# Other starting places in on-chip memory for two groups of operands of a packed attention and feed-forward kernel

## The chip, the core and the metric

The kernel runs on one core of a Trainium2 chip. Its time is the device time of one execution in microseconds (us). Three executions took 693.35, 694.07 and 694.8 us, so the median is 694.07 us. The core has a matrix engine (TensorE, PE in the profile; its weight loads have a row of their own, PEld), a vector engine (DVE), a scalar engine (ACT), a general engine (POOL) and a queue engine (SP), which here only starts transfers.

## What is computed

The inputs are q, k and v of 8 batches, 8 heads, 576 tokens and 64 values a head, 32 "pack" vectors p a head, and the matrices W_in (512 x 2048) and W_out (2048 x 512), all in 32 bits.

```
p_packed = softmax(scale * p @ k.T) @ v              # 32 rows a head
attn     = softmax(scale * q @ p_packed.T) @ p_packed
x        = attn with the heads side by side          # 4608 x 512
h        = x @ w_in
g        = h * (1 / (1 + exp(-h)))                   # SiLU
out      = g @ w_out                                 # 4608 x 512
```

The softmax adds 1e-9 to its sum. Nothing in the change touches the arithmetic.

## The kernel before

The second attention and W_in are merged. For each batch the pack vectors are first multiplied with W_in (the "packs times W_in", tiles `pw_hi` and `pw_lo`), and the hidden values h then come from the softmax shares `a2` times those. Every 32-bit operand of a large product is split into an upper part that TensorE's float32r type holds exactly and the lower remainder, and a product takes three matmuls: upper by upper, upper by lower, lower by upper.

Three kinds of matmul carry nearly all the work. Each is preceded by its own load of 128 columns of a stationary operand (128 x 128 values, 512 bytes in each partition), while the moving operand is streamed past it:

- **h, line 590.** 12 matmuls for a unit of two column blocks. The stationary operand is a slice of `pw_hi` or `pw_lo`, the moving one 288 columns of `a2_hi` or `a2_lo`. A tile of the packs has two halves, one for the even heads and one for the odd (`par` 0 and 1 in the code), each of 512 values. In a group of six matmuls the first three use half 0 and the last three half 1.
- **out, pairs, line 648 with 128 x 256.** For batches 2 to 7 the product with W_out is done by a scheme with seven products instead of eight for a pair of column blocks (`pair_products`). The stationary operands are seven parts of g (`g_hi` and `g_lo`, 7 x 128 values), the moving ones 256 columns of W_out or of sums of its blocks. A unit has 7 x 3 = 21 matmuls, and there are 96 units.
- **out, plain, line 648 with 128 x 512.** The first two batches use g without pairs, and the last 32 tokens of every half (the "rests") do so in all batches.

For a pair ACT writes g from PSUM (line 612), POOL makes the sums and differences (lines 622 to 624), ACT writes the upper parts (`all_upper`, line 638), DVE the lower parts (`all_lower`, line 642), and then TensorE may go on. A string, ORDER, sets the order of these steps on PE, DVE, ACT and SP by hand. A step named `Z0.` closes the pools of the early part and opens `pw_b` and `gp_main`, in which all g of the pairs lies.

Where a tile lies is set by the order in which pools are opened and by their sizes. I call the distance of an operand's first byte from the multiple of 256 bytes below it its *place*. All pools up to `gp_main` have sizes that are multiples of 256 bytes, at least between the big tiles, and so the tiles of W_out, of its sums, of the packs and of g itself begin at place 0. The slices that are used as operands are 512, 1024 or 2048 bytes apart and have the place of their tile. There are two exceptions: the second half of an `a2` tile begins 1152 bytes into it, at place 128; and `all_upper` puts the upper and lower parts of the pairs 56 values into their tile, at place 224 (for the rests it puts them at 0):

```
at = AT_G if g.shape[1] > FJ * P else 0          # line 634, AT_G = 56
both = [gp_main.tile([P, 7 * P + 64], F32R, name=name) for name in ("g_hi", "g_lo")]
```

Of the kernel before, what the change touches and what calls it, by code (L numbers as in the profile page):

```python
# [9 lines left out]
F32 = mybir.dt.float32  # L10
F32R = mybir.dt.float32r
# [8 lines left out]
P = 128  # L20
# [11 lines left out]
JW = DFF // NJ  # L32
FJ = JW // P
# [88 lines left out]

TP_BUFS = 4
EDGE = 504
AT_G = 56
ON_TOKENS = (0,)
SCALE = 1.0 / math.sqrt(D)
EPS = 1e-9
# [5 lines left out]
def packed_attention_ffn(ctx: ExitStack, tc: tile.TileContext, pkT, qT, v, w_in, w_out, out):  # L134
# [14 lines left out]
    ent = ctx.enter_context  # L149
    const = ent(tc.tile_pool(name="const", bufs=1))  # L150
    kvq = ent(tc.tile_pool(name="kvq", bufs=2))
    pw = ent(tc.tile_pool(name="pw", bufs=2))
# [29 lines left out]
    made = {}  # L182
# [39 lines left out]
    class Weights:  # L222
# [51 lines left out]
        def upper(self, n):  # L274
            hi, _ = self.both(n)
            nc.scalar.copy(hi, self.raw[n][1].bitcast(F32))
# [250 lines left out]
    class Packs:  # L527
# [18 lines left out]
        def upper(self):  # L546
            b, j = self.b, self.f // FJ
            if self.f % FJ == 0:
                pool = pw_b if b >= EARLY and j >= 2 else pw
                made["pw", b, j] = [pool.tile([P, 2, JW], F32R, name=name) for name in ("pw_hi", "pw_lo")]  # L550
            c = slice(self.f % FJ * P, (self.f % FJ + self.nf) * P)
            self.hi, self.lo = (t[:, :, c] for t in made["pw", b, j])
            nc.scalar.copy(self.hi, self.ps[:, :, : self.nf * P])
# [72 lines left out]
    def all_of(u):  # L626
        b, f, *more = units[u]
        if more:
            return rest[:, f : f + FJ].rearrange("p f e h s -> p (f e h s)")
        return hidden[u][:, P:]  # L630

    def all_upper(u):
        g = all_of(u)
        at = AT_G if g.shape[1] > FJ * P else 0
        both = [gp_main.tile([P, 7 * P + 64], F32R, name=name) for name in ("g_hi", "g_lo")]
        both = [t[:, at : at + g.shape[1]] for t in both]
        hidden[u] = g, *both
        nc.scalar.copy(both[0], g)  # L638
# [160 lines left out]
    def load_parts(b):  # L799
# [38 lines left out]
        "N": rest_values,  # L838
        "I": pair_sums,
        "F": all_upper,  # L840
        "L": all_lower,
        "O": lambda u: (rest_products if len(units[u]) > 2 else pair_products)(u),
# [13 lines left out]
    def early_done():  # L856
        nonlocal pw_b, gp_main
        scope.close()
        at_right[1].close()
        pw_b = ent(tc.tile_pool(name="pw_b", bufs=2, reuse_waits="tile"))  # L860
        gp_main = ent(tc.tile_pool(name="gp_main", bufs=2, reuse_waits="tile"))

    def weights_done():
# [7 lines left out]

    pw_b = gp_main = ring = tp = None
    steps |= {"Z0.": early_done, "Z1.": weights_done}
    for step in ORDER.split():
        which = step.rstrip("0123456789.") if step[0] != "Z" else step
# [44 lines left out]
```

## Time and profile before

| | |
|---|---|
| median of three executions | 694.07 us (693.35 to 694.8) |
| the profiled execution | 693.81 us, of which 692.0 us are the profile's span |
| TensorE busy | 672.5 us, 97% |
| DVE busy | 425.8 us, 62% |
| ACT busy | 387.0 us, 56% |
| POOL busy | 233.6 us, 34% |
| the chain that ended last | PE 76%, DVE 10%, ACT 5%, DMA 3% |

Durations of matmuls in the profile overlap: a matmul's row runs on while the next one has begun. How fast a stream of them goes is therefore read from starts in the timeline, or from the pieces of the chain of waits, which are merged by line and have a length and a count. A mean duration is of use only for comparing like with like.

### The profile page before, as it was taken

How to read it: one execution, taken by the hardware profiler on the slowest of the kernel's cores; microseconds unless marked ns; L12 is line 12 of the kernel's file. 1: busy time of each engine (PE TensorE's matmuls, PEld its weight loads, DVE VectorE, ACT ScalarE, POOL GpSimd, SP SyncE). 2: the span in 40 equal slices, each digit the busy share in tenths (PEclk: the TensorE clock that was granted, in tenths of full speed). 3: DMA queues.
4: the chain of work that ended last, by engine and by line, in shares of the span. 5: the costliest groups of instructions: out<-in, count | busy, mean ns of one | idle time of the engine just before them, and what ended most of it. 6: DMA issues, size and time to landing. Idle time of an engine off the chain costs nothing.

```text
span 692.0 us, 14725 instructions
## 1 busy us (share of the span) xinstructions
PE 672.5 (97%) x5958; PEld 591.5 (85%) x5958; DVE 425.8 (62%) x588; ACT 387.0 (56%) x641; POOL 233.6 (34%) x336
## 2 busy tenths in 40 slices
PE   7799999999999999999999999999999999999997
PEld 5477776788878998999888998899888898899995
DVE  5989989896774536753666425853665535663333
ACT  5787887463645535663556634755554754664431
POOL 1102054343203432544423343353251353435520
PEclk9899999999999999999999999999999999999999
DMA  9848864685967678967797578874994848685531
GB/s 362 328 136 307 282 222 173 235 267 184 386 242 283 247 245 329 363 251 262 283 342 282 184 284 308 348 279 131 353 353 168 303 132 307 265 313 190 212 139 45
DMA packets 55107, 178.62 MB, mean 258 GB/s; under 512 B 21760, under 2 KB 25856, under 8 KB 47360
## 3 DMA queue, kind: packets, MB, share of 16 engines
q1 hardware_dynamic: 54944, 177.56, 69.1%
q8 instruction: 47, 0.77, 0.4%
q10 hardware_dynamic: 96, 0.13, 0.1%
q14 instruction: 20, 0.16, 0.1%
HBM read 149.42 MB, written 24.12 MB: 251 GB/s over the span
## 4 chain that ended last, share of the span: by engine, by line
PE 76%; DVE 10%; ACT 5%; DMA 3%; issue 2%; POOL 2%; SPq 1%; ACTq 0%; DVEq 0%
PE ps_acc L648 45%; PE ps_two L590 23%; PE ps_two L287 5%; DMA win<-in_w_out 2%; PE ps_two L387 2%; DVE tm L423 1%; DVE g_lo L642 1%; DMA sums_of_w<-sums_of_w 1%; DVE g_lo L608 1%; DVE w_raw L252 1%; ACT g_hi L638 1%; DVE w_raw L256 1%; ACT g L612 1%; DVE wo_lo L280 1%; POOL g L623 1%
## 5 line engine op out<-in xcount | busy, mean ns | idle before, releaser
L642 DVE TENSOR_TENSOR g_lo<-g,g_hi 128x896 fp32r<-128x896 f32 x96 | 105.9, 1110 | 131.6 <-ACT g_hi L638 131.2
L648 PE MATMUL ps_acc<-wo_hi,g_hi 128*128 128x256 f32 (+1 forms) x576 | 184.7, 321 | 0.7 <-DVE o L790 0.7
L648 PE MATMUL ps_acc<-wo_hi,g_lo 128*128 128x256 f32 (+1 forms) x576 | 183.0, 318 | 2.2 <-DVE g_lo L608 2.2
L648 PE MATMUL ps_acc<-wo_lo,g_hi 128*128 128x256 f32 (+1 forms) x576 | 182.7, 317 | 0.0
L590 PE MATMUL ps_two<-a_hi,pw_hi 128*128 128x288 f32 x512 | 153.0, 299 | 1.5 <-DVE tm L423 1.5
L622 POOL TENSOR_TENSOR g<-g 128x128 f32<-128x128 f32 x96 | 56.2, 586 | 288.0 <-ACT g L612 287.9
L590 PE MATMUL ps_two<-a_lo,pw_hi 128*128 128x288 f32 x512 | 151.3, 295 | 0.0
L590 PE MATMUL ps_two<-a_hi,pw_lo 128*128 128x288 f32 x512 | 151.1, 295 | 0.0
L638 ACT CAST g_hi<-g 128x896 fp32r<-128x896 f32 x96 | 89.9, 942 | 77.6 <-POOL g L624 47.5
L648 PEld LDWEIGHTS ps_acc<-wo_hi,g_hi 128*128 128x128 f32 x576 | 108.1, 188 | 16.1 <-issue 5.6
L648 PEld LDWEIGHTS ps_acc<-wo_hi,g_lo 128*128 128x128 f32 x576 | 108.2, 188 | 12.4 <-DVE g_lo L608 4.7
L648 PE MATMUL ps_acc<-sums_of_w,g_hi 128*128 128x256 f32 x576 | 116.6, 284 | 0.0
L648 PEld LDWEIGHTS ps_acc<-wo_lo,g_hi 128*128 128x128 f32 x576 | 108.3, 188 | 6.8 <-DVE wo_lo L280 0.3
L590 PEld LDWEIGHTS ps_two<-a_hi,pw_hi 128*128 128x128 f32 x512 | 96.5, 188 | 14.4 <-PE ps_two L287 6.7
L590 PEld LDWEIGHTS ps_two<-a_lo,pw_hi 128*128 128x128 f32 x512 | 96.4, 188 | 0.8
L590 PEld LDWEIGHTS ps_two<-a_hi,pw_lo 128*128 128x128 f32 x512 | 96.5, 188 | 0.0
L648 PEld LDWEIGHTS ps_acc<-sums_of_w,g_hi 128*128 128x128 f32 x576 | 88.3, 188 | 8.9 <-issue 7.8
L648 PE MATMUL ps_acc<-sums_of_w,g_lo 128*128 128x256 f32 x288 | 80.5, 280 | 0.1
L623 POOL TENSOR_TENSOR g<-g 128x256 f32<-128x256 f32 x96 | 75.5, 787 | 6.6
L612 ACT ACTIVATE g<-ps_two 128x512 f32<-128x512 f32 x96 | 57.0, 598 | 33.4 <-DVE g_lo L642 16.8
L624 POOL TENSOR_TENSOR g<-g 128x128 f32<-128x128 f32 x96 | 53.2, 556 | 6.6
L648 PEld LDWEIGHTS ps_acc<-sums_of_w,g_lo 128*128 128x128 f32 x288 | 54.1, 188 | 0.4 <-DVE g_lo L642 0.3
(129 smaller groups left out, 799.7 us busy)
## 6 DMA issues: line engine op xcount, KB each, us to landing
sums_of_w<-sums_of_w SPq DMA_DIRECT2D x96, 768.0 KB, 6.2
w_quarter<-w_in SPq DMA_DIRECT2D x22, 1024.0 KB, 6.9
kvq_t<-in_v SPq DMA_DIRECT2D x8, 1280.0 KB, 8.8
kvq_t<-in_pkT SPq DMA_DIRECT2D x7, 1216.0 KB, 10.7
out<-o SPq DMA_DIRECT2D x16, 512.0 KB, 3.2
kvq_t<-in_qT SPq DMA_DIRECT2D x7, 1152.0 KB, 8.3
w_raw<-in_w_in SPq DMA_DIRECT2D x6, 1024.0 KB, 6.1
sums_of_w<-w_sums SPq DMA_DIRECT2D x8, 768.0 KB, 3.7
```

The costliest lines, as they stand in the source:

```text
L252: nc.vector.tensor_scalar(up.bitcast(F32), up.bitcast(F32), TOP, -TOP, op0=ALU.min, op1=ALU.max)
L256: nc.vector.scalar_tensor_tensor(low, up, -(2**31), low, op0=ALU.bitwise_and, op1=ALU.bitwise_or)
L287: nc.tensor.matmul(bank(par)[NP * i : NP * i + NP], lhs(r, i), rhs(r, i), start=True, stop=True)
L387: nc.tensor.matmul(self.ps[NP * i : NP * i + NP, par * D : par * D + D], e, vs[:n, c, h * D : h * D + D], start=(c == 0), stop=(c == 4),)
L590: nc.tensor.matmul(bank, p[:, par, cols], a[:, par], start=(n == 0), stop=(n == len(todo) - 1))
L612: nc.scalar.activation(g[:, : 4 * P].rearrange("p (e s) -> p e s", e=2), made["h", u, None][..., :MAIN], AF.Silu)
L622: nc.gpsimd.tensor_tensor(x[:, 4], x[:, 0], x[:, 2], ALU.subtract)
L623: nc.gpsimd.tensor_tensor(x[:, 5:7], x[:, 0:5:4], one, ALU.subtract)
L624: nc.gpsimd.tensor_tensor(x[:, 7], x[:, 3], x[:, 6], ALU.add)
L638: nc.scalar.copy(both[0], g)
L642: nc.vector.tensor_tensor(g_lo, g, g_hi.bitcast(F32), ALU.subtract)
L648: nc.tensor.matmul(out, g[:, rows], w, start=(first and n == 0), stop=(last and n == 2), skip_group_check=True)
```

## The change

It has three parts, all about places.

1. A pool "shift" of 64 bytes is opened before `gp_main`. Everything in `gp_main` moves on by 64 bytes: g of the pairs goes from place 0 to 64.
2. The room of 64 values in the tiles of the upper and lower parts goes. The parts of the pairs begin at the start of their tile, so at place 64 instead of 224. Those of the rests are put 48 values in, which is place 0 again (64 + 192 = 256), as before.
3. Each tile of the packs gets 32 values (128 bytes) of room behind each half. The first half stays at place 0, the second goes from place 0 to 128. A copy or a subtraction that writes both halves at once now writes two rows of 512 instead of one of 1024.

Tiles between the packs and `gp_main` (`a2`, `tm`, `o` and the small ones) move by 1024 bytes and keep their places. The list of instructions on each engine, their order and what they wait for are the same in both kernels, apart from the two-row shape in part 3 and one wait of ACT on its own earlier work, which is dropped.

```diff
-AT_G = 56
+AT_G = 16
+AT_PW = 32
...
-                made["pw", b, j] = [pool.tile([P, 2, JW], F32R, name=name) for name in ("pw_hi", "pw_lo")]
+                both = [pool.tile([P, 2 * JW + 2 * AT_PW], F32R, name=name) for name in ("pw_hi", "pw_lo")]
+                made["pw", b, j] = [t.rearrange("p (r n) -> p r n", r=2)[:, :, :JW] for t in both]
...
-        at = AT_G if g.shape[1] > FJ * P else 0
-        both = [gp_main.tile([P, 7 * P + 64], F32R, name=name) for name in ("g_hi", "g_lo")]
+        at = 0 if g.shape[1] > FJ * P else 64 - AT_G
+        both = [gp_main.tile([P, 7 * P], F32R, name=name) for name in ("g_hi", "g_lo")]
...
         pw_b = ent(tc.tile_pool(name="pw_b", bufs=2, reuse_waits="tile"))
+        ent(tc.tile_pool(name="shift", bufs=1)).tile([P, AT_G], F32, name="shift")
         gp_main = ent(tc.tile_pool(name="gp_main", bufs=2, reuse_waits="tile"))
```

## Rows read from the trace of the kernel before

**Rows 1.** The page: engines (busy us, share, instructions) and 40 slices.
```profile
PE 672.5 (97%) x5958; PEld 591.5 (85%) x5958; DVE 425.8 (62%) x588; ACT 387.0 (56%) x641; POOL 233.6 (34%) x336
...
PE   7799999999999999999999999999999999999997
...
PEclk9899999999999999999999999999999999999999
```

**Rows 2.** Windows before and after 215 us: busy us and instructions by engine.
```profile
0.00:215.00 215.00, 202.20 (x1632) 157.95 (x1633) 173.87 (x246) 137.87 (x233) 52.48 (x52) 0.98 0.71 264
215.00:692.00 477.00, 470.30 (x4328) 433.51 (x4326) 251.90 (x342) 249.13 (x408) 181.12 (x285) 1.00 0.69 256
```

**Rows 3.** Groups by shape: busy us, mean ns | idle before, releaser.
```profile
L590 PE MATMUL ps_two<-a_hi,pw_lo 128*128 128x288 f32 x512 | 151.1, 295 | 0.0
L648 PE MATMUL ps_acc<-sums_of_w,g_hi 128*128 128x256 f32 x576 | 116.6, 284 | 0.0
...
L648 PE MATMUL ps_acc<-wo_hi,g_hi 128*128 128x256 f32 x384 | 107.7, 281 | 0.0
L648 PE MATMUL ps_acc<-wo_lo,g_hi 128*128 128x256 f32 x384 | 107.5, 280 | 0.0
L648 PE MATMUL ps_acc<-wo_hi,g_lo 128*128 128x256 f32 x384 | 107.2, 279 | 0.0
...
L648 PE MATMUL ps_acc<-sums_of_w,g_lo 128*128 128x256 f32 x288 | 80.5, 280 | 0.1
```

**Rows 4.** The chain of waits, merged pieces: start us, length us, what, count.
```profile
193.18 5.49 PE ps_acc L648 x24
...
286.37 4.79 PE ps_two L590 x36
...
385.60 4.95 PE ps_acc L648 x42
```

**Rows 5.** Windows of line 590 alone: PE busy, PEld busy, with counts.
```profile
0.00:215.00 215.00, 59.24 (x408) 56.93 (x408) 0.98 0.71 264
215.00:692.00 477.00, 162.05 (x1128) 152.87 (x1128) 1.00 0.69 256
```

**Rows 6.** Timeline of PE, one unit of pairs after a short stop.
```profile
379.79 0.40 PE L648 MATMUL ps_acc<-sums_of_w,g_hi 128*128 128x256 f32 x2
...
382.12 0.28 PE L648 MATMUL ps_acc<-wo_hi,g_lo 128*128 128x256 f32 x1
382.24 0.30 PE L590 MATMUL ps_two<-a_hi,pw_hi 128*128 128x288 f32 x1
```

**Rows 7.** Groups in 403.68 to 403.82: the last matmuls of a pair, then the packs'.
```profile
L590 PE MATMUL ps_two<-a_hi,pw_hi 128*128 128x288 f32 x1 | 0.3, 297 | 0.0
L648 PE MATMUL ps_acc<-wo_hi,g_lo 128*128 128x256 f32 x1 | 0.3, 288 | 0.0
```

**Rows 8.** Groups in 385.25 to 385.50: the packs' last matmul before a pair.
```profile
L590 PE MATMUL ps_two<-a_hi,pw_lo 128*128 128x288 f32 x1 | 0.3, 294 | 0.0
```

**Rows 9.** Groups by shape: the copies and sums that read or write the moved tiles.
```profile
L642 DVE TENSOR_TENSOR g_lo<-g,g_hi 128x896 fp32r<-128x896 f32 x96 | 105.9, 1110 | 131.6 <-ACT g_hi L638 131.2
...
L638 ACT CAST g_hi<-g 128x896 fp32r<-128x896 f32 x96 | 89.9, 942 | 77.6 <-POOL g L624 47.5 <-PE ps_acc L648 28.0 <-issue 2.0
...
L622 POOL TENSOR_TENSOR g<-g 128x128 f32<-128x128 f32 x96 | 56.2, 586 | 288.0 <-ACT g L612 287.9
...
L556 DVE TENSOR_TENSOR pw_lo<-ps_two,pw_hi 128x1024 fp32r<-128x1024 f32 x31 | 37.6, 1212 | 11.3 <-ACT pw_hi L553 11.2
L553 ACT CAST pw_hi<-ps_two 128x1024 fp32r<-128x1024 f32 x31 | 31.4, 1014 | 32.1 <-PE ps_two L287 32.0
...
L642 DVE TENSOR_TENSOR g_lo<-rest,g_hi 128x512 fp32r<-128x512 f32 x16 | 11.6, 728 | 17.0 <-ACT g_hi L638 17.0
...
L638 ACT CAST g_hi<-rest 128x512 fp32r<-128x512 f32 x16 | 9.9, 621 | 17.9 <-PE ps_acc L648 17.8
```

## The prediction

> **What bounds the kernel now.** I read the page's engines first: PE is busy for 97% of the span, DVE for 62%, and the row of slices has PE at 9 nearly everywhere after the first two, and from the third on the granted clock is at nine tenths or more [rows 1]. Cut at 215 us, where the pairs begin, PE is busy for 470.30 of 477 us at a granted clock of 1.00, which is 2.4 GHz, and DVE and ACT for about 250 us each [rows 2]. In the groups of PE nothing waits: the idle time before the matmuls of the pairs and of the packs is 0.0 or 0.1 us [rows 3]. So from 215 us on the end is set by how closely TensorE's matmuls follow each other, and that is the only thing by which a change of places can move the time much.
>
> How closely they follow is read from the chain. 42 matmuls of 256 columns take 4.95 us, 117.9 ns each; 36 of 288 columns 4.79 us, 133.1 ns; 24 of 512 columns 5.49 us, 228.8 ns [rows 4]. From 288 to 512 columns that is 95.7 ns for 224 columns, 0.43 ns a column, or about one pulse of 2.4 GHz (0.417 ns). At one column a pulse the columns alone would be 106.7, 120.0 and 213.3 ns, so each matmul carries something on top: 11.2 ns where the stationary operand is a pair's part of g at place 224, 13.1 ns where it is a slice of the packs at place 0, and 15.5 ns with plain g at place 0. This surplus is what the change can act on. That it is smaller at place 224 is my reading; the three shapes differ in column count too, so the trace suggests it and doesn't prove it.
>
> Two more rows speak for it. The last matmul of a pair lasts 288 ns when the load behind it is of the packs, at place 0 [rows 7], against a mean of 279 for its group, nearly all of whose members have a load at place 224 behind them [rows 3]. And the last matmul of the packs lasts 294 ns when a load at place 224 follows [rows 8], against 295 in its group, where mostly loads at place 0 follow [rows 3]. So a matmul is slower by 1 to 9 ns while a stationary operand at place 0 is being loaded beside it. That isn't so everywhere: at 382.12 us the same neighbours start 0.12 us apart, like any two matmuls of a pair [rows 6]. Durations of equal shape differ as their starts do, since the tail after the columns is the same.
>
> **The change part by part.**
>
> *The pairs' parts from place 224 to 64.* 576 + 384 + 384 + 384 + 288 = 2016 matmuls [rows 3], all after 215 us, all on the path. No row shows a load at place 64. Bounds: at best the whole surplus goes, 11.2 ns x 2016 = 22.6 us gained; at worst place 64 is like place 0 behind 256 columns, 288 - 279 = 9 ns, 18.1 us lost. Between ends so far apart I go by the nearest row in which these matmuls run faster. After a short stop one unit ran from 379.79 to 382.24 us [rows 6]: 21 starts in 2.45 us, 116.7 ns each, 1.2 ns under the usual 117.9, with nothing but the moment of its beginning being different. So the usual stream holds a small stall that depends on how the loads fall beside the columns. I take 1.0 ns of it as gained at place 64: 2016 x 1.0 = 2.0 us.
>
> *The second halves of the packs from place 0 to 128.* Half of the matmuls of line 590 load from there; 1128 of the 1536 come after 215 us [rows 5], so 564 count, and the 204 in the early part are left at nothing, since there PE is idle for 13 of 215 us and DVE works for 174 [rows 2]. Bounds: the difference of the surpluses, 13.1 - 11.2 = 1.9 ns, either way, 1.1 us gained or lost. If place 0 itself is what costs, any other place helps, and I take the whole 1.9 ns: 1.1 us gained. The moving operand of these three matmuls lies at place 128 too, and the first three have 0 and 0, so both kinds get the same distance between their operands; the mean durations of the groups don't let me say whether that matters.
>
> *Copies and sums on the other engines.* ACT's copy to the parts takes 942 ns for 896 columns at place 224 and 621 ns for 512 at place 0 [rows 9]: 0.836 ns a column, and the same remainder of 193 ns for both. DVE's takes 1110 and 728 ns, 0.995 ns a column. Neither sees the place. POOL reads and writes g, which moves from 0 to 64, and no row has POOL at another place; it stands idle for 288.0 us waiting for ACT's g [rows 9], so even a tenth more on its 181.12 us [rows 2] would lie in idle time, unless a unit's g is already late. The two-row writes of the packs are 31 on ACT (1014 ns) and 31 on DVE (1212 ns) [rows 9]. Were each slower by a tenth, that is 3.1 and 3.8 us over the whole run, on engines with about 225 us free after 215 us, and the copy itself waits for PE [rows 9]. I put all this at nothing.
>
> *Sum.* -2.0 - 1.1 = -3.1 us. The profiled execution took 693.81 us, 1.8 us more than its span; it would take 690.7 us. The median of the runs is 0.26 us above the profiled one, so I predict 691.0 us. What is late next if PE is quicker is ACT's g for POOL and then DVE's lower part, 131.6 us of idle on DVE [rows 9]; at 3 us in 477 that cover holds.
>
> One rule speaks against any effect. The Trainium skill ("TensorE: Matmul & The Clock Gate", "Step-by-step: what each phase is for") says that TensorE reads the streamed operand and the weights through two independent ports, so that loading the next weights takes nothing from the running matmul. By it a place would change nothing and the time would stay at 694.1 us; what it doesn't explain is the matmul that lasts 288 instead of 279 ns when another operand is loaded beside it. The same page ("Back-to-back issue gap") gives 2.5 ns on top of the columns for a matmul alone; by that figure some 9 of the pairs' 11.2 ns would be open to gain, an estimate of 18 us. No run here shows a matmul without a load of its own.
>
> **The rivals.**
>
> *Nothing moves.* The surplus is 11 to 15 ns in all three shapes and could be the cost of changing the stationary operand, whatever its place. For it: the three shapes differ in columns and in destination, and the smaller surplus may belong to 256 columns. Against it: the 9 ns above. Time: 694.1 us, within 1.4 us.
>
> *Slower: only place 224 is good.* 224 is an odd multiple of 32 bytes, while 0, 64 and 128 are all multiples of 64. If what helps is that the load's reads fall half a 64-byte step beside the streamed ones, place 64 is as bad as place 0 and the gain that the pairs have now is lost, while the packs gain nothing. The price is at least the difference of the surpluses, 1.9 ns x 2016 = 3.8 us, so 697.9 us; with the 9 ns of the odd matmul it is 18 us, 712 us. For it: every good row here has place 224 and every bad one place 0, with moving operands at 0 and at 128 alike. Against it: nothing in the trace. It decides as soon as the pairs lose more than about 0.5 ns a matmul, since the packs' 1.1 us is all there is to set against it.
>
> *Much faster.* Place 64 is far from the beginning of a 256-byte stretch on both sides, 224 only 32 bytes from the next. If what costs is that load and stream pass such a beginning together, the pairs may lose half of their surplus: 5.6 x 2016 = 11.3 us, 682 us or so. For it: a stall of 1.2 ns that comes and goes with the moment of the start [rows 6]. Against it: the streams of half 1 of the packs, which pass their beginnings 128 bytes apart from the load's, show no lower duration than those of half 0 in the groups.
>
> **How the numbers follow.** I give 0.42 to the forecast (690 to 692.5 us or so), 0.08 to much faster, 0.22 to nothing moves and 0.28 to slower. A measurement of this kernel can tell about 0.2%, 1.4 us, from no change. So faster by more than that has 0.50, the same 0.22, slower 0.28. The range has to take in the lower price of the slower case with some of its tail and the beginning of much faster: 685 to 700 us. Left out are the larger gains (some 0.06) and prices above 3 ns a matmul (some 0.09). The likeliest case alone has 689 to 692.5 us.
>
> **What the profile will show.** If the steps are right, 42 matmuls of the pairs in one piece of the chain take 4.91 us or less instead of 4.95, and 36 of the packs 4.76 instead of 4.79; the means of the pairs' groups fall to about 279 ns and that of the packs to 294; the rows of ACT and DVE keep their durations. The slower case shows means of 282 ns or more for the pairs and the packs at 295. If the pairs' pieces are the same to 0.01 us and the time moves all the same, the cause is on another engine, POOL's sums first. I am wrong in the mechanism if the pairs and the packs don't move, and wrong in the sign if the pairs' surplus rises above 12 ns.

## The result and the profile after

The changed kernel takes 687.63 us (687.03 to 687.88, four runs) against 694.04 us (693.35 to 694.8) before: 0.9906 of the time, with a 95% interval of 0.9889 to 0.9923, so 6.4 us less. The forecast was 691.0 us. Direction and range held; the gain is twice what was forecast. The profiled execution took 687.03 us, its span 685.3.

The engines' row of the page after, then the windows up to and from 215 us (busy us and instructions by engine, in the order PE, PEld, DVE, ACT, POOL), to be read against [rows 1, 2]:

```profile
PE 665.6 (97%) x5958; PEld 584.8 (85%) x5958; DVE 427.0 (62%) x588; ACT 386.7 (56%) x641; POOL 232.1 (34%) x336
```

```profile
0.00:215.00 215.00, 202.74 (x1635) 158.97 (x1636) 175.21 (x246) 138.68 (x234) 52.09 (x53) 0.98 0.71 264
215.00:685.30 470.30, 462.89 (x4325) 425.83 (x4323) 251.75 (x342) 248.03 (x408) 180.02 (x284) 1.00 0.70 259
```

The first 215 us hold nearly the same work as before. The rest became 6.7 us shorter, from 477.0 to 470.3 us, and TensorE's busy time fell by 7.4 us in it, at the same granted clock. DVE, ACT and POOL are within 1.1 us of what they were. Where in TensorE's work the time went shows in the chain of waits (start us, length us, what, count), beside [rows 4]:

```profile
192.52 5.48 PE ps_acc L650 x24
...
284.82 4.79 PE ps_two L592 x36
...
383.50 4.77 PE ps_acc L650 x42
...
670.05 11.24 PE ps_acc L650 x48
```

42 matmuls of the pairs take 4.77 us, 113.6 ns each, where they took 4.95 us. 36 of the packs take 4.79 us as before, and 24 of 512 columns 5.48. Over all neighbouring starts of two pair matmuls, with stops left out, the mean fell from 117.75 to 114.17 ns, 3.6 ns; times 2016 that is 7.2 us. For the packs the mean of the whole run fell from 132.90 to 132.43 ns; after 215 us alone it fell from 132.86 to 132.64 ns, which over the 1128 late ones is 0.2 us. Of these 7.4 us together, 0.7 us are lost again in longer stops: TensorE is idle for 7.4 us of the later window instead of 6.7. The groups say the same (busy us, mean ns | idle before), beside [rows 3, 9]:

```profile
L592 PE MATMUL ps_two<-a_hi,pw_lo 128*128 128x288 f32 x512 | 152.1, 297 | 0.0
L650 PE MATMUL ps_acc<-sums_of_w,g_hi 128*128 128x256 f32 x576 | 115.0, 281 | 0.0
...
L650 PE MATMUL ps_acc<-wo_hi,g_lo 128*128 128x256 f32 x384 | 106.3, 277 | 0.0
...
L650 PE MATMUL ps_acc<-sums_of_w,g_lo 128*128 128x256 f32 x288 | 80.1, 278 | 0.3 <-DVE g_lo L644 0.3
...
L644 DVE TENSOR_TENSOR g_lo<-g,g_hi 128x896 fp32r<-128x896 f32 x96 | 106.1, 1113 | 128.3 <-ACT g_hi L640 128.0
...
L640 ACT CAST g_hi<-g 128x896 fp32r<-128x896 f32 x96 | 89.9, 941 | 76.1 <-POOL g L626 45.6 <-PE ps_acc L650 23.1 <-PE ps_two L288 2.3
...
L624 POOL TENSOR_TENSOR g<-g 128x128 f32<-128x128 f32 x96 | 56.2, 585 | 282.5 <-ACT g L614 282.4
...
L558 DVE TENSOR_TENSOR pw_lo<-ps_two,pw_hi 128x1024 fp32r<-128x1024 f32 x31 | 37.5, 1211 | 10.6 <-ACT pw_hi L555 10.6
L555 ACT CAST pw_hi<-ps_two 128x1024 fp32r<-128x1024 f32 x31 | 31.4, 1013 | 28.9 <-PE ps_two L288 28.9
```

The four groups of pairs that had 279 to 281 ns are at 277 and 278, the fifth went from 284 to 281. ACT, DVE and POOL keep their durations to 3 ns, at the new places and with the two-row writes.

For two of the kernels below, those with the parts at places 96 and 128, the profiled execution was disturbed, so only their times are used.

### The profile page after: what moved, and what is told of

Same layout as the page of the kernel before. It is cut to its first block, busy times and chain, and to the rows that moved or that the text cites. A ratio compares the mean times of both kernels' runs of the same rounds, so it can differ in the third digit from the quotient of the medians.

```text
span 685.3 us, 14725 instructions
## 1 busy us (share of the span) xinstructions
PE 665.6 (97%) x5958; PEld 584.8 (85%) x5958; DVE 427.0 (62%) x588; ACT 386.7 (56%) x641; POOL 232.1 (34%) x336
## 4 chain that ended last, share of the span: by engine, by line
PE 76%; DVE 11%; ACT 5%; DMA 3%; issue 2%; POOL 2%; SPq 1%; ACTq 0%; DVEq 0%
PE ps_acc L650 45%; PE ps_two L592 24%; PE ps_two L288 5%; DMA win<-in_w_out 2%; PE ps_two L388 2%; DVE tm L424 1%; DVE g_lo L644 1%; DVE g_lo L610 1%; DMA sums_of_w<-sums_of_w 1%; DVE w_raw L253 1%; ACT g_hi L640 1%; DVE w_raw L257 1%; DVE pw_lo L558 1%; ACT g L614 1%; DVE wo_lo L281 1%
## 5 line engine op out<-in xcount | busy, mean ns | idle before, releaser
L644 DVE TENSOR_TENSOR g_lo<-g,g_hi 128x896 fp32r<-128x896 f32 x96 | 106.1, 1113 | 128.3 <-ACT g_hi L640 128.0
L650 PE MATMUL ps_acc<-sums_of_w,g_hi 128*128 128x256 f32 x576 | 115.0, 281 | 0.0
```

The source lines that it names most:

```text
L644: nc.vector.tensor_tensor(g_lo, g, g_hi.bitcast(F32), ALU.subtract)
L650: nc.tensor.matmul(out, g[:, rows], w, start=(first and n == 0), stop=(last and n == 2), skip_group_check=True)
```

## The experiments

The theory after the result: the gain is the pace of the pairs' matmuls, and it depends on the place of the stationary operand that is loaded beside the stream. The rivals: g's own place, by way of the other engines; the packs; and, within the theory, whether the place alone counts or its distance from the place of the streamed operand.

### Which part carries it

**The parts alone**, in the kernel before:

```
-AT_G = 56
+AT_G = 16
```

> The kernel before with only the upper and lower parts of the pairs moved, from place 224 to place 64; g itself stays at place 0 and the packs stay whole. Theory: the whole gain is the start-to-start time of the pairs' matmuls, which fell by 3.6 ns x 2016 = 7.2 us between the two traces, and it comes from the place of the parts alone; then this kernel takes about 687.5 us and its pairs' pieces of 42 matmuls 4.77 to 4.78 us. Rival (g's own place, by way of ACT, POOL and DVE): 694 us, pieces of 4.95 us.

Measured: 687.94 us, 0.9929 (0.9912 to 0.9945). A piece of the chain:

```profile
382.89 4.78 PE ps_acc L648 x42
```

As the theory had it. With g still at place 0 and the packs whole, most of the gain is there, so g's own place is not the cause.

**Without the packs' room**, in the changed kernel:

```
-AT_PW = 32
+AT_PW = 0
```

> The changed kernel without the room between the halves of the packs (AT_PW = 0); g and its parts stay at place 64. Theory (all from the pairs): 687.5 to 688 us, since the packs' matmuls became only 0.5 ns x 1128 = 0.5 us quicker in the trace. Rival (the packs carry their forecast share of 1.1 us or more): 688.8 us or more.

Measured: 688.21 us, 0.9927 (0.9912 to 0.9942), between the theory's 688 and the rival's 688.8. The interval is 1 us wide to either side, so this run doesn't part the two.

**The packs' room, with the pairs at 224**, in the changed kernel:

```
-AT_G = 16
+AT_G = 56
```

> The changed kernel with g and its parts at place 224 (the shift is 224 bytes instead of 64) and the room between the halves of the packs left in. Theory (all from the pairs' place): 693 to 694.5 us, as before; pieces of 42 pair matmuls of 4.95 us. Rival (the packs' second half gives the forecast 1.1 us or more): 692.9 us or less.

Measured: 691.71 us, 0.9976 (0.9966 to 0.9985). This went against the theory: 1.6 us less than before. The two parts add up: 0.73% and 0.24% are 0.97%, and the whole change gave 0.94%. But the rival has less than half of it, as the steps of the packs and the chain of the pairs show:

```profile
383.78 4.90 PE ps_acc L650 x42
```

After 215 us the packs' own matmuls went from 132.86 to 132.21 ns, 0.7 us over 1128. The rest is in the pairs, whose place hadn't changed: their mean step fell from 117.75 to 117.15 ns, 1.2 us over 2016 (together 1.9 us, of which 1.6 reach the end). 4.90 us for 42 is 116.7 ns, the pace that one unit had in [rows 6]. Taken unit by unit, 13 of the 96 ran at about 117 ns before and 83 at 118; here 78 run at about 117. I read this as another rhythm of the same matmuls, into which the pairs fall when the packs before them end a little differently; no run shows that last step. (g itself lay at 224 here too; in the two runs above its place, 0 or 64, made no difference.)

### What the place does

**The parts at place 0**, in the kernel before (the next six have the same one-line edit, with AT_G = 32, 48, 8 and 24, and then 12 and 20):

```
-AT_G = 56
+AT_G = 0
```

> The kernel before with the upper and lower parts of the pairs at place 0 instead of 224. If place 0 is what costs, as the prediction had it, the pairs' matmuls take between 119.8 ns (the packs' surplus of 13.1 ns on 106.7) and 127 ns, 2.0 to 9 ns more than before: 698 to 712 us. If places 0 and 64 are alike because both are multiples of 64 bytes, it takes 687 to 688 us like the changed kernel.

Measured: 696.55 us, 1.0049 (1.0034 to 1.0064), below the forecast 698 and clearly slower than before.

```profile
386.00 5.03 PE ps_acc L648 x42
```

That is 119.8 ns, exactly the 106.7 ns of the columns and the packs' surplus of 13.1. So the reading that the packs and the pairs carry the same surplus at place 0 was right, and the upper figure of 127 ns, from one odd matmul, was not.

**Place 128:**

> The kernel before with the parts of the pairs at place 128. So far a pair's matmul takes 119.7 ns at place 0, 117.8 at 224 and 114.6 at 64. Theory 'midway': the load of the next stationary operand and the stream disturb each other when they pass the beginnings of 256-byte stretches together; the load goes at half the stream's pace, so in the time of one stretch of the load the stream passes two, and a load 128 bytes off falls on such a beginning again: 119 to 120 ns, 696 to 697 us, like place 0. Rival 'any place but 0': 114 to 117 ns, 687 to 692 us.

**Place 192:**

> The parts of the pairs at place 192. Theory 'midway': 192 is as far from a shared beginning as 64, so 114 to 115 ns and 687 to 688.5 us. Rival 'the nearer to the end of the stretch, the worse' (224 is worse than 64): about 117 ns, 692 us.

**Place 32:**

> The parts of the pairs at place 32. Theory 'midway': as far from a beginning as 224, so about 117 to 118 ns and 692 to 694 us. Rival 'the distance behind the multiple of 256 counts': between places 0 and 64, 116 to 118 ns, so this run alone does not part them; it gives the slope.

**Place 96:**

> The parts of the pairs at place 96. Theory 'midway': 32 bytes from the next bad place 128, like 224 and 32: 117 to 118 ns, 692 to 694 us. Rival 'any place of 64 bytes or more': 114 to 115 ns, 687 to 688.5 us.

**Places 48 and 80**, run last, to see whether the good place is broad:

> The kernel before with the parts of the pairs at place 48. Known: 32 gives 693.9 us and 118.1 ns, 64 gives 687.9 us and 114.6 ns, 96 gives 693.5 us. Theory 'a broad best place around 64': 114 to 116 ns, 687 to 690 us. Rival 'narrow, a step of 64 bytes is what fits': 117 to 118 ns, 692.5 to 694 us.

> The kernel before with the parts of the pairs at place 80. Theory 'broad': 114 to 116 ns, 687 to 690 us, and if the best place lies above 64, under 687 us. Rival 'narrow': 117 to 118 ns, 692.5 to 694 us.

| place of the parts | time, us | against before (95%) | 42 pair matmuls in the chain, us |
|---|---|---|---|
| 0 | 696.55 | 1.0049 (1.0034 to 1.0064) | 5.03 |
| 32 | 693.91 | 1.0009 (0.9998 to 1.0020) | 4.97 |
| 48 | 693.27 | 1.0001 (0.9990 to 1.0013) | 4.95 |
| 64 | 687.94 | 0.9929 (0.9912 to 0.9945) | 4.78 |
| 80 | 694.70 | 1.0018 (1.0008 to 1.0027) | 4.99 |
| 96 | 693.47 | 1.0002 (0.9992 to 1.0012) | not read |
| 128 | 694.88 | 1.0021 (1.0011 to 1.0030) | not read |
| 192 | 692.90 | 0.9998 (0.9989 to 1.0008) | 4.95 |
| 224 (before) | 693.33 to 694.13 | 1 | 4.95 |

Pieces at 48, 80, 192 and 32, one kernel each:

```profile
384.85 4.94 PE ps_acc L648 x42
```

```profile
386.32 4.99 PE ps_acc L648 x42
```

```profile
384.71 4.95 PE ps_acc L648 x42
```

```profile
384.61 4.97 PE ps_acc L648 x42
```

Of these places only 64 makes the kernel faster. Sixteen bytes to either side the whole gain is gone, and its mirror image 192 has the time of 224. The theory "midway" was right on 32 and 96, half right on 128 (slower than before, but 1.7 us short of place 0) and wrong on the times at 192, 48 and 80; it falls. "Any place but 0" falls with 128, and "broad" with 48 and 80.

The quick pace is not 64's alone, though. At place 192 three of the 96 units run at it, in two pieces that begin behind matmuls of line 287 and not behind the packs. These are the third and the last start of the longer piece (42 matmuls), 39 steps apart:

```profile
351.12 0.28 PE L648 MATMUL ps_acc<-sums_of_w,g_lo 128*128 128x256 f32 x1
...
355.54 0.28 PE L648 MATMUL ps_acc<-wo_hi,g_lo 128*128 128x256 f32 x1
```

That is 4.42 us, 113.3 ns a step. At place 64, with the parts alone moved, 80 of the 96 units have a mean step of 113 to 114 ns and 16 one of 118 ns; at 0, 32, 48, 80 and 224 no unit is below 116 ns. So the kernels differ not only in the pace of a unit, but also in how many units get the quick one.

**Everything moved by 64 bytes**, the streamed operands too:

```
 (the kernel before with AT_G = 16, and)
-    ident = const.tile([P, P + 352], F32, name="ident")
+    ident = const.tile([P, P + 368], F32, name="ident")
-EDGE = 504
+EDGE = 552
```

> The kernel before with the parts of the pairs 64 bytes behind g's tile places, and then every tile on chip moved on by 64 bytes: the parts at 128, all moving operands of the pairs at 64. Theory 'relative' (what counts is the place of the load against the place of the stream beside it): as with the parts alone at 64, pairs 114.6 ns and 687 to 688.5 us. Rival 'absolute' (the place of the load alone counts, and 128 gave 694.9 us): 694 to 696 us.

Measured: 689.07 us, 0.9930 (0.9915 to 0.9944), the ratio of the parts alone at 64. The parts lie at place 128 here, with the stream at 64:

```profile
384.58 4.78 PE ps_acc L648 x42
```

With the parts at 128 and the stream at 0 the time was 694.88 us. So it is the distance between the two places that counts, and the place by itself doesn't: 64 behind the stream is quick at both places of the stream that were tried (81 of the 96 units at 113 to 114 ns here, 80 with the parts alone). In the median this kernel is 0.6 us over its expectation; the kernel before, beside it, was 694.13 us, 0.8 us over that of the other comparison.

### Does the same distance help the other shapes?

**The rests**, in the changed kernel:

```
-        at = 0 if g.shape[1] > FJ * P else 64 - AT_G
+        at = 0
```

> The changed kernel with the rests' parts at place 64 too instead of 0; their moving operand has 512 columns from place 0. After 215 us about 153 of the 512-column matmuls are left, of which all are rests'. Theory (the same pair of places, 64 against 0, gives the same 5 to 6 ns as with the pairs, 119.7 to 114.2): 0.8 us less, 686.8 us; the 512-column start-to-start falls from 227 to about 222 ns. Rival (with more columns than the load takes, the surplus stays): 687.6 us.

Measured: 688.82 us, 0.9922 (0.9907 to 0.9937), 1.2 us over the changed kernel. The two intervals overlap, so the time alone doesn't show a loss; the end of the chain does:

```profile
671.44 11.47 PE ps_acc L650 x48
```

48 matmuls of 512 columns take 11.47 us instead of 11.24, 4.8 ns more each, and the median step of all the late ones went from 227 to 233 ns. Both theories are wrong: for 512 columns the distance of 64 bytes is worse than none.

**The packs at 64 and 192**, and **at 64 and 64**, in the changed kernel (the second takes the two halves, without room between them, from the 17th value of the tile on):

```
-made["pw", b, j] = [t.rearrange("p (r n) -> p r n", r=2)[:, :, :JW] for t in both]
+made["pw", b, j] = [t.rearrange("p (r n) -> p r n", r=2)[:, :, AT_PW // 2 : AT_PW // 2 + JW] for t in both]
```

```
-both = [pool.tile([P, 2 * JW + 2 * AT_PW], F32R, name=name) for name in ("pw_hi", "pw_lo")]
-made["pw", b, j] = [t.rearrange("p (r n) -> p r n", r=2)[:, :, :JW] for t in both]
+both = [pool.tile([P, 2 * JW + 2 * AT_PW], F32R, name=name)[:, AT_G : AT_G + 2 * JW] for name in ("pw_hi", "pw_lo")]
+made["pw", b, j] = [t.rearrange("p (r n) -> p r n", r=2) for t in both]
```

> The changed kernel with the packs' halves at places 64 and 192, which is 64 behind the place of their moving operand (0 and 128). Theory 'relative': each of the 1536 matmuls of 288 columns gains like the pairs, 133.3 to about 127.5 ns, so up to 6 us: about 682 us. Rival 'absolute, 64 alone is good': only the 768 of half 0 gain, 4 ns or so: 684.5 us. Rival 'only the pairs' shape gains': 687.6 us.

> The changed kernel with both halves of the packs at place 64, moving operands at 0 and 128. Theory 'relative': half 0 gains, half 1 (64 against 128) doesn't: about 684.5 us. Rival 'absolute': both gain, about 682 us. Rival 'only the pairs' shape gains': 687.6 us.

Measured: 688.03 us, 0.9911 (0.9895 to 0.9928), and 690.36 us, 0.9947 (0.9932 to 0.9962). The first is the last rival's case: 288 columns gain nothing from it. The second is slower than all three cases, and not by the packs:

```profile
285.59 4.76 PE ps_two L592 x36
...
384.20 4.95 PE ps_acc L650 x42
...
650.65 4.76 PE ps_acc L650 x42
```

In one kernel, with the same places throughout, pieces of pairs take 4.95 us or 4.76 us. The pairs have two rhythms even at the good distance. In this trace the matmuls just before tell which one follows. Of the 50 pieces that begin directly behind packs, 28 follow packs whose last six steps agree within 4 ns, and 26 of these run at 118 ns; 22 follow packs with uneven steps (126 to 137 ns), and 19 of these run at 113 to 114 ns. It isn't a rule for other kernels: with the parts alone at 64, 26 of 30 pieces behind even packs were quick. What it is in the matmuls before stays open.

**The packs at 96 and 224**, in the changed kernel, with 24 in place of AT_PW // 2 in the first of these two edits:

> The changed kernel with the halves of the packs at 96 and 224, 96 bytes behind the places of their moving operands. In the trace of before the one kind of 288-column matmul with a load 96 bytes behind its own moving operand (the last of the packs, before a pair) started its successor after 131 ns, against 133. If that holds for all 1536: 3 us less than the changed kernel, 684.5 us. Rival (for 288 columns all places are alike, as 64 and 192 were): 687.6 to 688.2 us.

Measured: 687.00 us, 0.9907 (0.9892 to 0.9921). The 3 us aren't there: it is the ratio of the changed kernel. No kernel here is better than the changed one by more than its interval.

## Why the prediction was right in direction and wrong in size

- **"What sets the end is how closely TensorE's matmuls follow each other."** Right. The 6.7 us of span all come from the window after 215 us, with the other engines unchanged.
- **The surplus is 13.1 ns at place 0 and 11.2 at 224.** Right as a reading across shapes: place 0 gave the pairs 119.8 ns, 13.1 over their columns.
- **"A matmul is slower by 1 to 9 ns while a stationary operand at place 0 is being loaded beside it."** It held in the kernel before and is no rule. Where packs follow a piece of pairs, its last matmul has the packs' first slice, at place 0, loaded beside it, and its own stream begins at place 0 too. Before, the next matmul starts 122.8 ns behind it (mean of 48), 5 ns more than within the pairs; with the parts at 0 it is 120.0 ns and in the changed kernel 113.9, no more than within their pairs (119.7 and 114.2). The load beside it is the same each time; what differs is the pairs' own operands and the rhythm up to there. Within a unit the load beside a matmul and the matmul's own stationary operand have the same place, so no run here parts the two.
- **The pairs' parts, 1.0 ns x 2016 = 2.0 us.** This is the step that failed, in its size. Measured: 3.6 ns on average, 4.3 in a full piece, and the part alone took 0.71 to 0.73% off the time, about 5 us. I took the nearest row in which the same matmuls ran faster, the 116.7 ns of [rows 6]. It was misread, too: that unit doesn't follow a stop, and more than its moment is different. Matmuls of 512 columns run right up to it, where other units have the packs before them:

```profile
379.55 0.40 PE L648 MATMUL ps_acc<-wo_hi,g_lo 128*128 128x512 f32 x1
```

So the 116.7 ns show a second rhythm at the same place, which most units have once the packs get their room (4.90 us for 42), and not a measure of what a better place gives. The best place goes below it, to 113.6 ns. The sweep shows that rows at 0 and 224 could not have given the size: seven other places, 48 and 80 among them, gave times within 0.5% of before, and 117.6 to 119.8 ns where a row was read. The best case of this term, 22.6 us, contained it, and so did the range. That the direction came out right is in part luck: no row had place 64, and the seven other places gave no gain.
- **"If place 0 itself is what costs, any other place helps."** Wrong as a rule. What counts is the distance between the place of the load and that of the streamed operand, shown by moving both; and of the distances tried only 64 bytes made the kernel faster, though three units at 192 reached the same pace.
- **The packs, 1.9 ns x 564 = 1.1 us.** Near in its sum, wrong in its way. The room between the halves gave 1.6 us by itself, some 0.7 of it in the packs' matmuls and the rest in the pairs behind them, which no term had. In the changed kernel the packs' late matmuls gained 0.2 us, 36 of them took 4.79 us and not 4.76, and the mean duration in their groups rose (295 to 297 ns) while their steps became shorter. So "durations of equal shape differ as their starts do" doesn't hold to a nanosecond or two, and 294 against 295 ns proved nothing.
- **Copies and sums at nothing.** Right: 941, 1113, 585, 1013 and 1211 ns, where they had 942, 1110, 586, 1014 and 1212 [rows 9].
- **The rivals.** "Nothing moves" fell: the place of the load alone moved the pairs' pace from 119.8 to 113.8 ns. The Trainium skill ("TensorE: Matmul & The Clock Gate", "Step-by-step: what each phase is for") says that weights and stream are read through two independent ports and a load takes no read bandwidth from the running matmul; that a place then changes nothing, as the prediction drew from it, isn't so in these traces. "Only place 224 is good" fell with 64, though 0 and 128 are bad as it said. "Much faster" was nearest in the pairs, 11.3 against 7.2 us where the forecast had 2.0, but not in the time (682 us); its mechanism, a shared passing of the 256-byte beginnings, fell with the times at 192, 48 and 80.

Open: why 64 bytes behind gives most units the quick pace and 64 bytes before (place 192) only three, why 512 columns lose by what 256 gain from, and what it is in the matmuls before a unit that picks its rhythm. It is open, too, whether the place counts of the operand that is loaded beside a matmul or of the one that the matmul uses. No run here tells these apart.

## What to carry to other kernels

Where a stream of matmuls with a load each is the bound and takes more time than its columns, move the stationary operand in steps of 16 bytes against the streamed one and measure each place: it costs some bytes of room and was worth 0.7% here for the pairs alone. Do it for each shape apart, since the place that is best for one was bad for another, and look at the steps unit by unit, since a place can have the quick pace in few units or in most. And don't forecast such a gain from rows at other places: they showed that 224 is better than 0, and nothing of 64.

## What was not expected of the hardware

- A load 64 bytes behind its stream takes 6 ns off a matmul of 256 columns here against a load at the same place (119.8 to 113.8 ns), and 16 bytes more or less undo most of it (117.9 and 118.8 ns).
- The same 64 bytes cost a matmul of 512 columns 4.8 ns (11.24 to 11.47 us for 48).
- A stream of equal matmuls can run at two paces within one kernel, with the same places throughout: 4.95 and 4.76 us for 42.
